# An mLSTM cell fused with a max-of-two MLP on one core: a hand-written engine order, the relu form, spread next-group work, and a denominator that is checked instead of applied

## Chip, cores, metric

One core of one Trainium2 chip. The metric is the device time of one execution in microseconds (us). A profile's span runs from the first to the last instruction of one execution; in these runs the device time is 1.6 to 2.2 us longer than the span of the same execution. Five engines work from their own queues, each in its own order: TensorE (PE in the profile, its weight loads PEld), VectorE (DVE), ScalarE (ACT), POOL, and SP, which issues most loads. PSUM is the memory in which the program puts TensorE's results, in banks. The granted clock is the share of TensorE's full clock that the profile records as let through; "half clock" is 0.5 of it. A run is called slow when its time is over 1.5% above that of the fastest run of the same kernel; comparisons use the fast runs.

## The reference, cut to what matters

```python
def _attn_ref(q, k, v, i_gate, f_gate, o_gate):        # 4 batches, 8 heads, 768 tokens, head size 40
    for t in range(S):
        m_new = np.maximum(f_gate[:, :, t] + m, i_gate[:, :, t])
        f_stab = np.exp(f_gate[:, :, t] + m - m_new); i_stab = np.exp(i_gate[:, :, t] - m_new)
        C = f_stab[..] * C + i_stab[..] * (v_t outer k_t)
        n = f_stab[..] * n + i_stab[..] * k_t
        denom = np.maximum(np.abs(n . q_t), 1.0)
        y[:, :, t] = sigmoid(o_gate) * (C q_t) / denom
def _moe_ref(x, w1, w2, w_out):                        # x: 3072 x 320, w1 and w2: 320 x 1024
    return np.maximum(x @ w1, x @ w2) @ w_out
```

## The kernel before

Only the first 64 tokens of each batch put anything into the state (a flag at the end checks it and starts a general path if not). So each batch has one small state, and every tile of 128 tokens is: transposes of q, four small matmuls (`ph`), the gate and the normaliser on VectorE and POOL (`y`), transposes of y (`py`). I call this the front of a tile. Four tiles make a group: `up` multiplies it by w1 - w2 in two halves, ScalarE takes the absolute value, and `out` sums the result. Since max(a, b) = (a + b)/2 + |a - b|/2, the half sum is folded into one small matrix Wc = (w1 + w2) w_out / 2. The framework's scheduler orders the instructions of every engine.

```python
def h_tile(b, c, P=None):
    ...                                            # four matmuls into ph
    nc.vector.tensor_scalar(out=den, in0=ph[:, :, D], scalar1=-1.0, scalar2=1.0, op0=OP.mult, op1=OP.max)
    nc.vector.tensor_tensor(out=den, in0=ph[:, :, D], in1=den, op=OP.max)
    nc.vector.reciprocal(out=rec, in_=den)
    nc.vector.tensor_tensor(out=t, in0=ph[:, :, 0:D], in1=sig[b][:, c], op=OP.mult)
    nc.gpsimd.tensor_tensor(out=y[:, 0:DM]..., in0=t, in1=rec..., op=OP.mult)
    nc.gpsimd.tensor_copy(out=y[:, DM:DM + 64], in_=y[:, DM - 64:DM])      # completes y
def moe_u(g, half):
    ...                                            # 8 full and 4 half-height matmuls of 512 columns
        nc.scalar.activation(out=gts[g][:, f:f + 2, :], in_=pus[lo], func=AF.Abs)
def moe_out(g, s):                                 # 3 matmuls with Wc, 8 with wo, copy, store
    ...
for g in range(1, NG + 1):
    for n in pairs: ...; front(n)                  # two pairs of tiles of group g
    for half in range(2):
        if g < NG: moe_u(g, half)
        for s in range(2): moe_out(g - 1, half * 2 + s)
# cut: loads, gates, state(b), weights, the check, the general path
```

## Time and profile before

| | before |
|---|---|
| device time, median of the first 3 runs | 136.48 us (136.3 to 137.49) |
| span of the profiled execution | 138.1 us |
| TensorE busy | 102.4 us, 74% |
| mean granted TensorE clock | 0.988 |

The table by stages comes first (kernel before). Its columns are the stretch, its length, the busy time of PE, PEld, DVE, ACT and POOL with the number of instructions, the granted TensorE clock, the DMA share and GB/s.

```profile
core 0: us, PE busy (x) PEld busy (x) DVE busy (x) ACT busy (x) POOL busy (x), PEclk, DMA share, GB/s
15.00:20.00 5.00, 2.39 (x17) 1.61 (x18) 5.00 (x5) 2.58 (x4) 4.03 (x3) 1.00 1.14 287
25.00:30.00 5.00, 2.75 (x26) 2.32 (x27) 3.78 (x12) 2.30 (x1) 3.98 (x7) 1.00 1.12 282
35.00:40.00 5.00, 4.95 (x37) 2.82 (x35) 4.00 (x9) 0.32 (x1) 0.98 (x3) 1.00 1.07 290
50.00:55.00 5.00, 2.99 (x19) 1.41 (x18) 2.01 (x9) 0.00 (x0) 3.06 (x7) 0.86 0.12 41
55.00:60.00 5.00, 4.65 (x23) 2.14 (x23) 0.62 (x3) 1.10 (x2) 0.00 (x0) 0.80 0.11 36
80.00:85.00 5.00, 4.53 (x44) 2.52 (x40) 2.89 (x11) 1.94 (x2) 1.88 (x4) 1.00 0.08 29
```

TensorE has little to do until 30 us while DMA runs at its limit; from 35 us on it is busy nearly all the time, but for the stretch around 50 to 60 us. The clock column starts at 1.00 only because no clock was recorded there (the record of this trace begins at 36.6 us): matmuls of 320 columns start 0.29 us apart at 32 us and 0.136 us apart later. The next lines are waits (waiting instruction, arrow, what ended the wait: total us, times, longest).

```profile
ACT L163 <- DMA ost<-in_o_gate_dram: 12.2, 1, 12.2
PEld L260 <- POOL y L250: 9.3, 16, 1.8
PE py L260 <- POOL y L250: 3.8, 8, 1.6
```

ScalarE's first table load stood 12.2 us behind its own DMA issues, which delayed the gates' exponentials to 13.5 us; their transposes then stood on TensorE until 18.8 us, behind transposes of weights that waited for POOL's sums. In the steady part TensorE waits for POOL's y. The last lines are TensorE's work in order of time (start, duration, instruction, count): some stalled y transposes and the first matmuls of `up` for groups 1 to 5.

```profile
32.09 2.31 PE L300 MATMUL pwc<-wo,wsT 128*128 128x320 bf16 x8
53.33 0.28 PE L260 MATMUL py<-ident_b,y 128*128 128x128 bf16 x2 [0.45 <-POOL y L250]
54.16 0.29 PE L260 MATMUL py<-ident_b,y 128*128 128x128 bf16 x1 [0.41 <-POOL y L252]
55.84 0.63 PE L315 MATMUL pu<-xT_165,wd 128*128 128x512 bf16 x1
74.22 1.89 PE L315 MATMUL pu<-xT_166,wd 128*128 128x512 bf16 x7
91.13 1.89 PE L315 MATMUL pu<-xT_167,wd 128*128 128x512 bf16 x7
105.28 1.89 PE L315 MATMUL pu<-xT_168,wd 128*128 128x512 bf16 x7
121.28 1.89 PE L315 MATMUL pu<-xT_169,wd 128*128 128x512 bf16 x7
```

From group 2 to group 5 the starts are 15.7 us apart on average, (121.28 - 74.22)/3.

### The profile page before, as it was taken

How to read it: one execution, taken by the hardware profiler on the slowest of the kernel's cores; microseconds unless marked ns; L12 is line 12 of the kernel's file. 1: busy time of each engine (PE TensorE's matmuls, PEld its weight loads, DVE VectorE, ACT ScalarE, POOL GpSimd, SP SyncE). 2: the span in 40 equal slices, each digit the busy share in tenths (PEclk: the TensorE clock that was granted, in tenths of full speed). 3: DMA queues.
4: the chain of work that ended last, by engine and by line, in shares of the span. 5: the costliest groups of instructions: out<-in, count | busy, mean ns of one | idle time of the engine just before them, and what ended most of it. 6: DMA issues, size and time to landing. Idle time of an engine off the chain costs nothing. (4 is left out here: it accounts for less than half of the span.)

```text
span 138.1 us, 2120 instructions
## 1 busy us (share of the span) xinstructions
PE 102.4 (74%) x761; PEld 57.4 (42%) x767; DVE 72.7 (53%) x196; ACT 37.4 (27%) x41; POOL 42.8 (31%) x87
## 2 busy tenths in 40 slices
PE   0000163568999876998899999997989999999870
PEld 0000042455734543345564445643654456543540
DVE  6980799767581992017694246634582156520220
ACT  0004820600059700055013550005500550014400
POOL 7530758794154026000541005414031005500000
PEclk9999999999999997799999999999999999999999
DMA  5999999999979911110112002110012101210041
GB/s 113 237 280 298 288 268 359 257 307 194 320 186 261 298 52 52 47 47 0 47 47 100 0 0 95 47 52 0 0 52 100 47 0 47 95 47 5 2 147 57
DMA packets 29407, 16.77 MB, mean 121 GB/s; under 512 B 17552, under 2 KB 28304, under 8 KB 29392
## 3 DMA queue, kind: packets, MB, share of 16 engines
q1 hardware_dynamic: 23152, 14.62, 37.1%
q10 hardware_dynamic: 6240, 1.97, 7.4%
q8 instruction: 8, 0.13, 0.4%
q14 instruction: 7, 0.06, 0.1%
HBM read 12.65 MB, written 3.93 MB: 120 GB/s over the span
## 5 line engine op out<-in xcount | busy, mean ns | idle before, releaser
L324 ACT ACTIVATE gt<-pu 128x1024 bf16<-128x1024 f32 x24 | 23.3, 1022 | 57.9 <-PE pu L320 57.9
L250 POOL TENSOR_TENSOR y<-t,rec 128x320 bf16<-128x320 f32 x24 | 17.3, 723 | 64.5 <-DVE den L244 45.1
L334 PE MATMUL po<-wo,gt 128*128 128x320 bf16 x192 | 33.7, 302 | 0.3 <-ACT gt L324 0.2
L334 PEld LDWEIGHTS <-gt 128*128 128x128 bf16 x192 | 17.5, 98 | 8.3 <-ACT gt L324 1.3
L336 DVE COPY o_sb<-po 128x320 f32<-128x320 f32 x24 | 11.2, 474 | 17.3 <-PE po L334 17.2
L282 PE MATMUL pw<-ident_b,ws 128*128 128x128 bf16 x16 | 2.6, 307 | 19.4 <-POOL ws L274 19.4
L260 PE MATMUL py<-ident_b,y 128*128 128x128 bf16 x72 | 11.8, 240 | 5.8 <-POOL y L250 3.8
L315 PEld LDWEIGHTS <-wd 128*128 128x128 bf16 x96 | 9.3, 99 | 12.1 <-issue 4.0
L206 DVE COPY qT<-pq 128x1024 bf16<-128x1024 bf16 x12 | 8.2, 686 | 7.5 <-PE pq L204 7.4
L260 PEld LDWEIGHTS <-y 128*128 128x128 bf16 x72 | 5.5, 104 | 14.8 <-POOL y L250 9.3
L248 DVE TENSOR_TENSOR t<-ph,sig 128x320 f32<-128x320 f32 x24 | 11.5, 481 | 0.0
L195 ACT ACTIVATE sig<-ost 128x960 f32<-128x960 f32 (+2 forms) x9 | 7.8, 917 | 9.3 <-issue 7.5
L282 PEld LDWEIGHTS <-ws 128*128 128x128 bf16 x16 | 1.4, 130 | 20.1 <-POOL ws L274 20.1
L236 PE MATMUL ph<-cq,qT 128*128 128x82 bf16 x80 | 6.0, 212 | 1.4 <-DVE qT L206 1.4
L252 POOL COPY y<-y 128x64 bf16<-128x64 bf16 x24 | 5.8, 240 | 1.5
L236 PEld LDWEIGHTS <-qT 128*128 128x128 bf16 x80 | 4.5, 105 | 3.6 <-DVE qT L206 2.3
L189 DVE CAST qb_128<-qst 128x960 bf16<-128x960 f32 x4 | 4.5, 1135 | 2.4 <-PE pq L204 2.4
L274 POOL TENSOR_TENSOR ws<-w_0_98,w_0_103 128x512 bf16<-128x512 f32 x2 | 3.4, 1726 | 6.6 <-DMA w_0_103<-in_moe_w_dram 6.6
L189 DVE CAST qb_127<-qst 128x960 bf16<-128x960 f32 (+2 forms) x5 | 5.2, 1037 | 0.3 <-DMA qst<-in_q_dram 0.3
L204 PE MATMUL pq<-ident_b,qb_127 128*128 128x128 bf16 x48 | 5.3, 265 | 0.0
L243 DVE TENSOR_SCALAR den<-ph 128x8 f32<-128x8 f32 x20 | 3.1, 160 | 4.0 <-PE ph L236 3.8
L274 DVE TENSOR_TENSOR wd<-w_0_98,w_0_103 128x512 bf16<-128x512 f32 x2 | 2.4, 1222 | 4.8 <-DMA w_0_103<-in_moe_w_dram 4.8
(110 smaller groups left out, 148.5 us busy)
## 6 DMA issues: line engine op xcount, KB each, us to landing
out_dram<-o_sb SPq DMA_DIRECT2D x24, 160.0 KB, 1.8
qst<-in_q_dram SPq DMA_DIRECT2D x3, 800.0 KB, 5.7
ost<-in_o_gate_dram SPq DMA_DIRECT2D x3, 800.0 KB, 7.3
wo_st<-in_moe_w_out_dram SPq DMA_DIRECT2D x1, 1280.0 KB, 6.9
w_0_98<-in_moe_w_dram SPq DMA_DIRECT2D x1, 512.0 KB, 5.3
w_0_103<-in_moe_w_dram SPq DMA_DIRECT2D x1, 512.0 KB, 7.6
w_1_110<-in_moe_w_dram SPq DMA_DIRECT2D x1, 512.0 KB, 7.4
w_1_115<-in_moe_w_dram SPq DMA_DIRECT2D x1, 512.0 KB, 5.7
```

What stands on the lines that cost most here:

```text
L189: eng.tensor_copy(out=qb[b % 2][:, c0:c1, :, 0:D], in_=qst[b][:, :, c0:c1, :].rearrange("p h c d -> p c h d"))
L195: nc.scalar.activation(out=sig[b][:, c0:c1], in_=ost[b][:, :, c0:c1, :].rearrange("p h c d -> p c h d"), func=AF.Sigmoid)
L206: nc.vector.tensor_copy(out=qT[b][:, c0:c0 + 2], in_=pq)
L236: nc.tensor.matmul(ph[:, 2 * p:2 * p + 2, :].rearrange("p a b -> p (a b)"), lhsT, rhs, start=True, stop=True)
L248: nc.vector.tensor_tensor(out=t, in0=ph[:, :, 0:D], in1=sig[b][:, c], op=OP.mult)
L250: nc.gpsimd.tensor_tensor(out=y[:, 0:DM].rearrange("p (h d) -> p h d", d=D), in0=t, in1=rec.unsqueeze(2).to_broadcast([128, H, D]), op=OP. ...
L252: nc.gpsimd.tensor_copy(out=y[:, DM:DM + 64], in_=y[:, DM - 64:DM])
L260: nc.tensor.transpose(py[:, c, j * L:(j + 1) * L], y[:, c * 128:(c + 1) * 128], ident_b)
L315: nc.tensor.matmul(pus[lo][:, j, :], wd[:, c, f * 128:(f + 1) * 128], x[:, c, :], start=(c == 0), stop=False)
L324: nc.scalar.activation(out=gts[g][:, f:f + 2, :], in_=pus[lo], func=AF.Abs)
L334: nc.tensor.matmul(po, gt[:, f, s * L:(s + 1) * L], wo[:, f, :], start=False, stop=(f == NFF - 1))
L336: nc.vector.tensor_copy(out=o_sb, in_=po)
```

## The change

Its parts: every engine's order is written by hand (`manual_schedule`), not left to the scheduler; max(a, b) = b + relu(a - b), so Wc = w2 w_out and POOL's sums become casts; the normaliser is no longer applied: the kernel only records n.q and checks at the end that |n.q| never exceeds 1, and takes the general path if it does, so what it saves holds only for inputs like these; next group's front is cut into six slots placed between `up` and the output tiles; 29 dummy matmuls fill early gaps to keep the clock up; the half-height matmuls of Wc run in pairs. Staging gets three buffers, and ScalarE issues only two loads.

```diff
+    order.enter_context(tc.manual_schedule())
+    idle(9)                                    # dummy matmuls; also idle(4) and idle(16)
-        nc.vector.reciprocal(out=rec, in_=den)
-        nc.gpsimd.tensor_tensor(out=y[:, 0:DM]..., in0=t, in1=rec..., op=OP.mult)
+        nc.vector.tensor_tensor(out=ys[n][:, 0:DM]..., in0=ph[:, :, 0:D], in1=ost[b][:, :, c, :], op=OP.mult)
+        nc.gpsimd.tensor_copy(out=ys[n][:, DM:DM + 64], in_=ys[n][:, DM - 64:DM])
+        nc.vector.tensor_copy(out=nqb[:, n, :], in_=ph[:, :, D])      # for the check
-            nc.scalar.activation(..., func=AF.Abs)
+            nc.scalar.activation(..., func=AF.Relu)
+    wc_mm()
+    start_batch(1)
+    for i in range(6):
+        slot(i, 0)                             # fronts of tiles 6 and 7, nothing between
     for g in range(1, NG + 1):
         for half in range(2):
             if g < NG:
-                moe_u(g, half)
-            for s in range(2):
-                moe_out(g - 1, half * 2 + s)
+                up(g, half)
+            if g == 1 and half == 1:
+                start_batch(2)                 # POOL: casts of q, first gate; ScalarE: sigmoids
+            out_rows(g - 1, half * 2)
+            slot(half * 3, g)
+            out_full(g - 1, half * 2)
+            slot(half * 3 + 1, g)
+            out_full(g - 1, half * 2 + 1)
+            slot(half * 3 + 2, g)
# cut: the slots' contents, loads, weights, the check
```

## The prediction

> **What bounds the kernel now.** Until about 37 us TensorE waits for loads and the prologue: the table by stages has it busy 2.4 to 2.8 us of each 5 us from 15 to 30 us, the DMA share is about 1.0 until 45 us, and the wait list shows ScalarE's first table load standing 12.2 us behind its own DMA issues. Matmuls run at half pace there (128x320 starts 0.29 us apart at 32 us, 0.136 later). From 37 to 133.6 us TensorE is the bound: 4.2 to 5.0 us busy of each 5, except around 50 to 55 us, where transposes wait for POOL's y and the granted clock then falls to 0.5 for 3.4 us. The last output copy starts at 133.7 us; the span ends at 138.1.
>
> **Floor of the steady part**, from start-to-start times in the timeline at full clock: an up half is 8 x 0.234 + 0.54 = 2.4 us; an output tile 11 x 0.136 = 1.5; a pair's q transposes 0.46, its ph matmuls 0.32, its y transposes 0.34 (six unstalled took that; three stalled took 0.36); state about 0.55 per batch. A group of four tiles with its successor's front is 4.8 + 6.0 + 2.2 + 0.4 = 13.4 us. The starts of up for groups 2 to 5 are 15.7 us apart: 2.3 us per group is stall.
>
> **What the change does.**
> - To y: den, max, reciprocal (about 0.5 us DVE a tile) and POOL's 0.72 us multiply go; DVE's 0.48 us multiply writes y at once. With fronts placed half a group ahead, y stalls should vanish: estimate 2 us per group, 8 us over four.
> - Relu should cost what Abs does on ScalarE (1.02 us), off the path. POOL's sums of weights become casts. Half-height Wc matmuls run in pairs; the switch eats what they save.
> - Prologue: gates ready near 8 us instead of 20.5; the first three pairs finish during the weight loads. Dummies keep the clock up; worth 1 to 2 us at most, since loads set that time.
> - Cost: output of group 0 now waits for up of group 1, which needs batch 1 loaded. Wo landed at 25 us; batch 1 is another 2.1 MB, at 272 GB/s (25 to 48 us) landing about 32.8 us. Sigmoid of its rest (about 1.6 us), y, transposes and copy put up of group 1 at about 37 us, against 55.8 before, with group 0's output still owed. TensorE idles several us before it, so its clock falls and the start loses about 2 us. The Trainium skill, "TensorE: Matmul & The Clock Gate", Part 1, says an idle window of about 3.4 us halves the clock; the trace's stretch at 0.5 has that length.
>
> **Sum.** 37 + 2 (cold) + 4 x 13.7 + 10.8 (up of group 5, output of 4) + 5.9 (last output) + 4.4 (tail, as now) = 115 us of profile span. Timed runs are about 1.2% below the profile (136.5 against 138.1): **113.5 us, 80% range 107 to 120**. Chances: faster over 2% 0.97, within 2% 0.02, slower 0.01.
>
> **Right if the profile shows:** gate transposes near 8 us; up of group 1 at 34 to 40 us, its y waiting for batch 1's ost; half clock just before; then up starts 13.4 to 14 us apart, TensorE 95% busy or more, no y waits; POOL under 30 us, DVE near 60.
>
> **Wrong if:** the fixed order makes TensorE wait for DVE (o_sb, qT, xT share one queue), groups staying above 14.5 us; batch 1 lands much later or earlier; the clock falls in mid-run; or POOL's casts of q hold the transposes.

## The result, and the profile after

| | before | after |
|---|---|---|
| device time, median (4 runs each) | 136.99 us (136.3 to 139.61) | 125.34 us (124.58 to 125.64) |
| span of the profiled execution | 138.1 us | 123.4 us |
| TensorE busy | 102.4 us, 74% | 103.7 us, 84% |
| VectorE, POOL busy | 72.7, 42.8 us | 57.7, 34.1 us |

The ratio of times is 0.916 (95% interval 0.911 to 0.922). Ratios here are the mean time of one kernel's fast runs over that of the other's of the same rounds, so not quite the ratio of the medians. The kernel is faster, but 12 us slower than predicted and outside the range.

The table by stages, kernel after:

```profile
15.00:20.00 5.00, 4.07 (x39) 2.66 (x37) 3.33 (x11) 1.14 (x2) 0.71 (x3) 1.00 1.07 303
35.00:40.00 5.00, 2.92 (x36) 2.15 (x34) 3.39 (x8) 2.22 (x3) 2.28 (x4) 1.00 1.10 330
40.00:45.00 5.00, 4.45 (x22) 1.86 (x22) 1.50 (x4) 0.00 (x0) 0.25 (x2) 0.66 1.14 234
50.00:55.00 5.00, 3.98 (x33) 2.06 (x31) 1.88 (x6) 3.00 (x4) 0.69 (x2) 1.00 0.09 33
55.00:60.00 5.00, 2.91 (x23) 1.96 (x24) 1.39 (x3) 0.72 (x1) 1.78 (x5) 0.85 0.10 36
85.00:90.00 5.00, 5.00 (x48) 3.40 (x45) 2.63 (x6) 1.94 (x2) 0.24 (x1) 1.00 0.10 34
```

The steady part is now full (85 to 90 us), the prologue fuller, and holes are left at 35 to 45 us and 50 to 60 us. TensorE's work in order of time, kernel after: Wc and then the way to `up` of group 1, and the starts of `up` for groups 2 to 5, then the half-height matmuls of the last group.

```profile
32.64 3.43 PE L321 MATMUL pwc<-wo,w2T 128*128 128x320 bf16 x24
36.81 0.61 PE L225 MATMUL pq<-ident_b,qb 128*128 128x128 bf16 x8 [0.36 <-DVE kT L234]
38.20 0.38 PE L247 MATMUL ps<-qT,kT 128*128 128x128 bf16 x4 [0.78 <-DVE qT L227]
39.37 0.33 PE L259 MATMUL ph<-vw,P 128*128 128x82 bf16 x4 [0.63 <-DVE P L249]
40.34 0.69 PE L275 MATMUL py<-ident_b,y 128*128 128x128 bf16 x6 [0.64 <-DVE y L262]
41.68 3.44 PE L335 MATMUL pu<-xT,wd 128*128 128x512 bf16 x8 [0.20 <-DVE xT L277]
60.77 2.46 PE L335 MATMUL pu<-xT,wd 128*128 128x512 bf16 x8
74.19 1.89 PE L335 MATMUL pu<-xT,wd 128*128 128x512 bf16 x8
89.14 1.89 PE L335 MATMUL pu<-xT,wd 128*128 128x512 bf16 x8
101.32 1.89 PE L335 MATMUL pu<-xT,wd 128*128 128x512 bf16 x8
112.51 0.29 PE L351 MATMUL po<-Wc_t,xT 64*128 64x320 bf16 x1 [0.34 <-DVE o_sb L362]
```

`up` of group 1 starts at 41.7 us after waits of 0.36, 0.78, 0.63, 0.64 and 0.20 us, and then takes 3.44 us for what takes 1.89 later: the clock is at half. The last line is from the last group: the second half-height matmul starts 0.65 us after the first, of which 0.34 us is waiting for VectorE to empty the PSUM bank into `o_sb` (runs 11, 12, 14 and 15 change that). The second hole, all engines in order of time, kernel after:

```profile
52.00 1.94 ACT L344 ACTIVATE gt<-pu 128x1024 bf16<-128x1024 f32 x2 [4.37 <-PE pu L340]
53.82 1.90 ACT L208 ACTIVATE ost<-ost 128x320 f32<-128x320 f32 x2
54.37 0.72 POOL L212 TENSOR_TENSOR ost<-ost,gT 128x320 f32<-128x320 f32 x1 [4.31 <-ACT ost L208]
55.04 1.38 POOL L204 CAST qb<-qst 128x640 bf16<-128x640 f32 x2
56.37 0.41 POOL L264 COPY y<-y 128x64 bf16<-128x64 bf16 x2
56.66 0.41 PE L275 MATMUL py<-ident_b,y 128*128 128x128 bf16 x4 [2.68 <-POOL y L264]
58.14 1.98 PE L360 MATMUL po<-wo,gt 128*128 128x320 bf16 x8
```

The y copies of tiles 10 and 11 wait in POOL's queue behind batch 2's gate multiply and casts, and that multiply waits for a sigmoid that stands behind the Relus on ScalarE. TensorE waits 2.68 us, and the output that follows takes 1.98 us where eight such matmuls take 1.25.

**Where the 14.7 us of span came from.** Before, at the start of `up` for group 2 (74.2 us) the output of groups 0 and 1 was done. After, at the same point (60.8 us) that of group 1 was still owed, about 5.9 us. So about 7.5 us come from before that point (74.2 - 60.8 - 5.9) and about 7.1 us from after it.

### The profile page after: what moved, and what is told of

Same layout as the page of the kernel before. It is cut to its first block, busy times and chain, and to the rows that moved or that the text cites. A ratio compares the mean times of both kernels' runs of the same rounds, so it can differ in the third digit from the quotient of the medians.

```text
span 123.4 us, 2122 instructions
## 1 busy us (share of the span) xinstructions
PE 103.7 (84%) x797; PEld 60.7 (49%) x797; DVE 57.7 (47%) x152; ACT 39.7 (32%) x47; POOL 34.1 (28%) x80
## 4 chain that ended last, share of the span: by engine, by line
PE 57%; DVE 4%; ACT 2%; POOL 2%; issue 1%; DVEq 0%
PE po L360 21%; PE pu L335 16%; PE po L358 5%; PE pu L340 4%; PE pq L225 3%; PE py L275 3%; PE ph L259 2%; DVE o_sb L362 2%; ACT gt L344 2%; PE po L351 1%; DVE xT L277 1%; POOL qb L204 1%; DVE y L262 1%; POOL ost L212 1%; PE pc L239 1%
## 5 line engine op out<-in xcount | busy, mean ns | idle before, releaser
L344 ACT ACTIVATE gt<-pu 128x1024 bf16<-128x1024 f32 x24 | 23.3, 1022 | 59.1 <-PE pu L340 59.1
L335 PE MATMUL pu<-xT,wd 128*128 128x512 bf16 x96 | 24.8, 405 | 1.4 <-DVE wd L289 1.2
L262 DVE TENSOR_TENSOR y<-ph,ost 128x320 bf16<-128x320 f32 x24 | 11.6, 487 | 18.2 <-PE ph L259 15.6
L165 PE MATMUL pd<-warm,ident_b 128*128 128x512 bf16 x29 | 9.5, 492 | 1.4 <-POOL ident_f masks.py:197 1.4
L225 PE MATMUL pq<-ident_b,qb 128*128 128x128 bf16 x96 | 8.8, 241 | 2.1 <-POOL qb L204 1.0
L358 PE MATMUL po<-Wc_t,xT 128*128 128x320 bf16 x48 | 10.5, 300 | 0.0
L204 POOL CAST qb<-qst 128x640 bf16<-128x640 f32 (+1 forms) x12 | 8.1, 696 | 5.9 <-DMA qst<-in_q_dram 5.7
L225 PEld LDWEIGHTS <-qb 128*128 128x128 bf16 x96 | 7.3, 110 | 3.3 <-issue 1.5
L208 ACT ACTIVATE ost<-ost 128x320 f32<-128x320 f32 (+1 forms) x8 | 7.7, 1001 | 3.3 <-DMA ost<-in_o_gate_dram 3.3
L277 DVE COPY xT<-py 128x768 bf16<-128x768 bf16 x12 | 6.6, 551 | 4.0 <-PE py L275 4.0
L340 PE MATMUL pu<-xT,wd 64*128 64x512 bf16 x48 | 7.3, 381 | 0.0
```

What stands on the lines that cost most here:

```text
L165: nc.tensor.matmul(pd[:, 0, :], ident_b, warm, start=True, stop=True)
L204: f(out=qb[b % 2][:, c0:c1, :, 0:D], in_=qst[b][:, :, c0:c1, :].rearrange("p h c d -> p c h d"))
L225: nc.tensor.transpose(pq[:, j, p, :], qb[b % 2][:, c + j, 2 * p:2 * p + 2, :].rearrange("p a b -> p (a b)"), ident_b)
L262: nc.vector.tensor_tensor(out=ys[n][:, 0:DM].rearrange("p (h d) -> p h d", d=D), in0=ph[:, :, 0:D], in1=ost[b][:, :, c, :], op=OP.mult)
L335: nc.tensor.matmul(pus[lo][:, j, :], wd[:, c, f * 128:(f + 1) * 128], x[:, c, :], start=(c == 0), stop=False)
L340: nc.tensor.matmul(pus[lo][:, j, :], wd2[r, half, j * 128:(j + 1) * 128], x[r, 2, :], start=False, stop=True)
```

## The experiments

The kernel after is the base of every run unless said. Each shares its rounds with the kernel before, so all are compared by that ratio: after stands at 0.916. The kernel before was itself not the same in all rounds: its median was 137.1 us in the rounds of runs 1 to 4 and 9 to 12, 137.4 in those of 5 to 8, and 139.0 in those of 13 to 15, where ratios therefore flatter by about 1%. The intervals reach 0.7 to 1.8 us to each side, so differences of 1 to 2 us between runs are at the edge of what this can tell. Every kernel gave a correct result.

### 1. The copy that completes y moves to VectorE

```diff
-        nc.gpsimd.tensor_copy(out=ys[n][:, DM:DM + 64], in_=ys[n][:, DM - 64:DM])
+        nc.vector.tensor_copy(out=ys[n][:, DM:DM + 64], in_=ys[n][:, DM - 64:DM])
```

> The 64-column copy that completes y goes from POOL to VectorE; nothing else changes. Theory A (the 2.7 us wait of the y transposes at 53.9 us comes from POOL's strict order: the copy stands behind batch 2's gate multiply and q casts; the half clock after it, 3.4 us, is a consequence): both go, the start of up for group 2 comes 4 us earlier, the time is 125.3 - 4 = 121 us. Theory B (VectorE's queue, with 24 more small copies, is the next limit, or another wait takes its place, such as batch 2's data): the time falls by less than 1.5 us.

Measured: 121.2 and 122.1 us in two fast runs, 127.2 and 129.2 us in two slow ones (ratio of fast runs 0.886). The wait at 53 us was gone, but the profile, of a slow run, showed a longer prologue. In it VectorE's copy stands still while POOL works. The first of two views is VectorE in order of time, of this run:

```profile
19.20 0.18 DVE L264 COPY y<-y 128x64 bf16<-128x64 bf16 x1
22.84 3.01 DVE L264 COPY y<-y 128x64 bf16<-128x64 bf16 x1
```

The second is POOL in order of time, of the same run:

```profile
22.58 1.06 POOL L448 MEMSET qb<- 128x1152 bf16 x1
23.57 1.38 POOL L449 MEMSET kblk<- 128x1536 bf16 x1
24.89 0.92 POOL L450 MEMSET vw<- 128x984 bf16 x1
```

0.18 us alone, 3.01 us when three POOL memsets run: the copy ends when they do. That such waits make the whole of the longer prologue (`up` of group 0 starts at 31.3 us, not 24.3) is likely and not shown. So this run does not decide; run 13 repeats it without that collision.

### 2. The slots of each half run together

```diff
             slot(half * 3, g)
-            out_full(g - 1, half * 2)
             slot(half * 3 + 1, g)
-            out_full(g - 1, half * 2 + 1)
             slot(half * 3 + 2, g)
+            out_full(g - 1, half * 2)
+            out_full(g - 1, half * 2 + 1)
```

> In each half group the three slots of next-group work run together before the two output tiles, not between them. Theory A (spreading hides the VectorE and POOL hops between TensorE steps): each half now exposes about 1.5 to 2 us, over eight halves with work 10 us or more: 135 us or above. Theory B (the queue of TensorE and two PSUM buffers would hide most of it anyway): below 129 us.

Measured: 133.8 us, ratio 0.975 (0.968 to 0.981). Near theory A: in a fixed order the spread is worth about 8 us.

### 3. The same program, ordered by the scheduler

```diff
-    order.enter_context(tc.manual_schedule())
```

> The hand-written order is given up: the same program, with the tool's own scheduler free to reorder, as in the kernel before. Theory A (the order itself carries most of the 11.6 us gain): 131 us or more, with y waits and up periods near 15 us. Theory B (less work per tile, earlier gates and staging carry it): within 3 us of 125.3.

Measured: **114.9 us**, ratio 0.837 (0.832 to 0.842). Both theories fall: the fixed order is not the gain, it costs 10.4 us. The starts of `up` for groups 1 and 2, TensorE, this run:

```profile
39.76 0.30 PE L359 MATMUL po<-wo,gt 128*128 128x320 bf16 x1
40.16 0.57 PE L359 MATMUL po<-wo,gt 128*128 128x320 bf16 x3
41.92 1.89 PE L334 MATMUL pu<-xT,wd 128*128 128x512 bf16 x8
53.03 1.89 PE L334 MATMUL pu<-xT,wd 128*128 128x512 bf16 x8
```

Group 1 starts no earlier (41.9 us), but output of group 0 (`po`) runs in the gaps before it, no half clock follows (the granted clock is 1.00 from 22.6 to 111 us), and group 2 starts at 53.0 us, not at 60.8.

### 4. The denominator applied again, in the hand-written order

```diff
+        nc.vector.tensor_scalar(out=den, ...); nc.vector.tensor_tensor(out=den, ...)
+        nc.vector.reciprocal(out=rec, in_=den)
-        nc.vector.tensor_tensor(out=ys[n]..., in0=ph[:, :, 0:D], in1=ost[b][:, :, c, :], op=OP.mult)
+        nc.vector.tensor_tensor(out=t, in0=ph[:, :, 0:D], in1=ost[b][:, :, c, :], op=OP.mult)
+        nc.gpsimd.tensor_tensor(out=ys[n]..., in0=t, in1=rec..., op=OP.mult)
# cut: the check of |n.q|, its copy per tile, and POOL's first multiply per batch (sig_first) go out
```

> The normaliser is computed and applied for each tile again (three VectorE operations, reciprocal, POOL multiply), in the hand-written order; the check of it goes. Theory A (as predicted: the long chain to y is what stalled transposes, 2 us per group): 125.3 + 8 or so = 133 us. Theory B (the spread slots hide the longer chain in the steady part, only the unhidden prologue, two batches deep, pays about 1.2 us per pair): 125.3 + 3 to 5 = 129 us.

Measured: 135.2 us in the one fast run, about 138 in three slow ones. That is about 10 us above after, so theory A, and more; with one fast run the size is rough. The edit lengthens the chain to y and also gives POOL more to do (47.4 us in place of 34.1); the two are not separated. Almost all of the change's gain over the kernel before is gone.

### 5. Wc woven into the fronts of tiles 6 and 7

```diff
-    wc_mm()
-    for i in range(6):
-        slot(i, 0)
+    f_k(1); wc_mm(0); f_c(1); f_q(6); wc_mm(1); f_s(1); f_h(7)
+    wc_mm(2); f_h(6); f_q(8); f_y(6)          # wc_mm(c): one of three blocks
```

One of Wc's copies also moves from ScalarE to VectorE.

> Hand-written order kept, but the three eight-matmul blocks of Wc are placed between the front steps of tiles 6 and 7, where TensorE stood idle; loads unchanged. Theory A (the start of up for group 1 at 41.7 us is set by a chain of front steps with nothing between them, after Wc, and by the clock that falls in its gaps): up starts near 38.5 us at full clock, the time is 125.3 - 4.5 = 121 us. Theory B (as predicted: batch 1's loads set it): start and time stay within 1 us.

Measured: 121.3 us, ratio of the three fast runs 0.883 (0.870 to 0.896). Theory A in time; `up` of group 1 starts at 39.8 us, not at the 38.5 that was expected. ScalarE's sigmoid of batch 1 also starts earlier, at 34.3 us in place of 36.4, since the Wc copies no longer stand before it; the run does not separate the two. TensorE at `up` of group 1, and at the second hole, which is untouched:

```profile
39.78 1.90 PE L335 MATMUL pu<-xT,wd 128*128 128x512 bf16 x7 [0.65 <-DVE xT L277]
53.23 0.61 PE L275 MATMUL py<-ident_b,y 128*128 128x128 bf16 x4 [2.67 <-POOL y L264]
```

### 6. An extra load ahead of batch 1

```diff
+    for j in range(4):
+        spare = outp.tile([128, DM], FP, name="o_sb", tag="o_sb")
+        nc.sync.dma_start(out=spare, in_=moe_w_out[128 * j:128 * j + 128])
     load_batch(1, nc.sync)
```

> Four extra loads of 164 KB (0.66 MB, about 2.4 us at 272 GB/s) go into the queue ahead of batch 1. Theory B (batch 1's loads bound the start of up for group 1): start and time 2.4 us later, 127.7 us. Theory A (the order's chain binds, the data lies waiting): under 0.7 us.

Measured: 125.8 us, ratio 0.919; `up` of group 1 starts at 42.15 us, 0.5 us later, not 2.4, and `up` of group 0 was already 0.5 us later in this execution (24.76 against 24.30). Theory A: loads did not set that start. The loads were delayed indeed: the last one of batch 1 landed at 36.0 us in place of 32.4. ScalarE in order of time, kernel after, shows where its data lay waiting:

```profile
36.11 0.43 ACT L322 CAST Wc_t<-pwc 128x320 bf16<-128x320 f32 x1 [1.75 <-PE pwc L321]
36.43 1.90 ACT L208 ACTIVATE ost<-ost 128x320 f32<-128x320 f32 x2
```

The sigmoids of batch 1 start only after Wc's last copy, 4 us after their data.

### 7. No dummies

```diff
-    idle(9)
-    idle(4)
-        if half == 0:
-            idle(16)
-        else:
+        if half == 1:
```

> All 29 dummy matmuls are taken out. As predicted (worth 1 to 2 us, since loads bound the prologue): 125 to 127.5 us. Rival: prologue matmuls are on the chain, and without dummies they run at half clock until about 36 us (up of group 0 twice 1.9 us, Wc 3.4, transposes 1 us): 125.3 + 6 to 8 = 132 us. Third: the 16 before up of group 0 only delay it: 124 us.

Measured: 125.8 us, ratio 0.916, the same as after. Without dummies the first `up` half runs at half clock (3.2 us in place of 1.9) but starts 1.4 us earlier, at 22.9 us; what the dummies win they had cost. The second half starts at 29.6 us (29.0 with dummies), in both after 1.18 us of waiting for VectorE or ScalarE to prepare its weights. Nor did the first 13 dummies always keep the clock up: in the profiles of runs 5, 6 and 13 it is recorded at half from 8 or 9 us to 18 or 19 us.

### 8. The Abs form put back

```diff
-            f(out=w2b[:, c, half * 512:half * 512 + 512], in_=t[:, 1, c])
+            G.tensor_tensor(out=w2b[:, c, ...], in0=t[:, 0, c], in1=t[:, 1, c], op=OP.add)
-            A.copy(out=wo[:, 0:4], in_=wo_st[:, 0:4])
+            A.activation(out=wo[:, 0:4], in_=wo_st[:, 0:4], func=AF.Copy, scale=0.5)
-            nc.scalar.activation(..., func=AF.Relu)
+            nc.scalar.activation(..., func=AF.Abs)
```

> The Abs form is put back in the hand-written order: POOL adds w1 and w2 (1.3 to 1.7 us per 128x512) where ScalarE and POOL cast w2; wo is halved in its cast; Relu becomes Abs. Theory A (the relu form shortens the prologue, since sums on POOL hold the transposes before Wc): 3 to 6 us slower, 129 us. Theory B (sums hide behind other prologue waits): within 1.5 us of 125.3.

Measured: 127.2 us, ratio 0.927 (0.916 to 0.939). About 1.5 us slower; the interval reaches down to no difference. It falls between the two theories. In its profile Wc starts at 35.2 us, not 32.6.

### 9 and 10. Denominator applied, and slots bunched, both in the scheduler's order

The edits are those of runs 4 and 2, with `manual_schedule` taken out as in run 3.

> Denominators applied per tile again (as in the fourth run) and the scheduler free to reorder (as in the third, 114.9 us). Theory A (the long chain to y costs what it adds wherever no other TensorE work is ready; a scheduler cannot hide it, as in the kernel before): 121 us or more. Theory B (with free order the chain is hidden, and the 10 us it cost in the hand-written order was that order's inflexibility): 118 us or less.

> Slots of next-group work written together in the program (as in the second run, 133.8 us), the scheduler free to reorder. Theory A (the spread in the text matters only because a fixed order keeps it): within 2 us of 114.9. Theory B (the scheduler follows the text's order closely, so the spread is worth its 8.5 us here too): 121 us or more.

Measured: 123.5 us, ratio 0.901 (0.896 to 0.905), for the denominator; 116.4 us, ratio 0.850 (0.845 to 0.855), for the bunched slots. The denominator costs 8.7 us of 137 in the scheduler's order too (0.901 - 0.837), so neither of the two orders hides it; that is theory A of run 9. The spread, worth 8 us in the fixed order, is worth about 1.8 us when the scheduler may move things (0.850 - 0.837); that is theory A of run 10.

### 11. Three mends at once

Runs 1 and 5 together, and in the last group:

```diff
-            out_rows(g - 1, half * 2)                  # half-height matmuls of both tiles
+            out_rows(g - 1, half * 2, (0,) if g == NG else (0, 1))
...
+            if g == NG: out_rows(g - 1, half * 2, (1,))
             out_full(g - 1, half * 2 + 1)
```

> The hand-written order with three mends: Wc woven into the fronts of tiles 6 and 7 (4 us alone), the copy that completes y on VectorE (3.5 us alone), and in the last group the half-height matmuls of one tile at a time, so that the second does not wait 0.65 us twice for a PSUM bank (1.3 us). If the three causes are separate and complete: 125.3 - 8.8 = 116.5 us, up starts of groups 1 and 2 about 14 us apart. If the half-clock stretches have another cause, or mends overlap: 119 us or more.

Measured: 123.7 us median, 121.5 and 123.1 us in fast runs, two slow ones (ratio of fast runs 0.903). A miss: the prologue had grown again. `up` of group 0 starts at 28.7 us, not 24.3, with copies of 0.9 us on VectorE beside POOL's work.

### 12. The scheduler's order without dummies

Run 3, with run 7's edit and the last group's half-height matmuls one tile at a time.

> The scheduler's order (114.9 us), without the dummies and with the last group's half-height matmuls one tile at a time. Dummies bought nothing in the hand-written order; in the scheduler's their 12 us of TensorE time stands among real work until 23 us. Theory A (loads and chain bind the prologue): 113 to 115 us. Theory B (the clock matters here, where up of group 0 and Wc are followed by output at once): 116.5 us or more.

Measured: **112.4 us**, ratio 0.822 (0.816 to 0.827), the fastest kernel. The two edits together are worth about 2 us (0.837 - 0.822); they are not separated. Runs 14 and 15 show no worth of dummies in the hand-written order.

### 13. The copy on VectorE only from tile 8 on

```diff
-        nc.gpsimd.tensor_copy(out=ys[n][:, DM:DM + 64], ...)
+        (nc.vector if n >= 8 else nc.gpsimd).tensor_copy(out=ys[n][:, DM:DM + 64], ...)
```

> As the first run, but the completing copy moves to VectorE only for tiles 8 to 23; the prologue keeps POOL. Theory A (POOL's queue holds y of tile 11 behind batch 2's work, and the half clock follows from that idle stretch; the first run's longer prologue came from VectorE and POOL in each other's way): prologue as before (up of group 1 near 42 us), no wait of 2.7 us, up of group 2 near 56.5 us, all runs at 125.3 - 4 = 121.3 us, no slow ones. Theory B (the wait moves elsewhere or VectorE copies slow the groups): above 123.5 us.

Measured: 121.1 us, ratio 0.878 (0.868 to 0.888), all four runs fast. Theory A. `up` of group 1, the y transposes and `up` of group 2:

```profile
42.40 1.89 PE L335 MATMUL pu<-xT,wd 128*128 128x512 bf16 x7 [0.20 <-DVE xT L277]
52.88 0.50 PE L275 MATMUL py<-ident_b,y 128*128 128x128 bf16 x6
56.07 1.89 PE L335 MATMUL pu<-xT,wd 128*128 128x512 bf16 x7
```

No wait before the transposes, no half clock after them; group 1 takes 13.7 us (56.07 - 42.40), as the prediction had it. But the first line shows luck as well: the half clock at `up` of group 1 is missing too, though nothing before it was changed. By their mean clocks, two of the four executions most likely had it (0.943; 121.6 and 122.0 us) and two did not (0.956; 120.4 and 120.6 us). The first two are the ones to set against the three executions of after with both half clocks (125.2 to 125.6 us): the copy is worth about 3.7 us, and the rest of the 4.2 is where the clock's windows fell.

### 14 and 15. The mends together without the collision, with and without dummies

Runs 5 and 13 and the last group's edit of run 11; run 15 also without dummies.

> The three mends together (Wc woven in, copy on VectorE from tile 8 on, last group's half-height matmuls one by one), dummies kept. If the three causes are separate and complete: 125.3 - 4.0 - 4.0 - 1.3 = 116 us. If they overlap or another wait appears: 119 us or more.

> The same without dummies. Theory A (dummies buy and cost nothing, as in the hand-written order before): within 1 us of the run with them. Theory B (they delay: the 16 before up of group 0 end 1.3 us after its weights are ready; as the scheduler's order gained about 2 us without them): 1 to 2 us faster.

Measured: 116.9 us, ratio 0.845 (0.836 to 0.853), and 117.1 us, ratio 0.846 (0.836 to 0.855). The times add up within 1 us: 125.3 - 4.0 - 4.2 - 1.3 would be 115.8. The 1.3 us for the last group is read from the trace (0.65 us twice) and was never run alone, and run 14's profile has no half clock at `up` of group 1. Dummies again make no difference: theory A of run 15.

## Why the prediction was right or wrong

Right:

- **Direction and the steady groups.** Groups 2 to 4 take 13.5 us on average ((101.32 - 60.77)/3) against 15.7 before; 13.7 was forecast. One by one they take 13.4, 15.0 and 12.2 us, where 13.4 to 14 was forecast for each. TensorE is busy 97% of that time, and no group of them waits for y as before.
- **The denominator.** Runs 4 and 9 put it, chain to y and POOL's multiply together, at about 9 us in either order; 8 us was forecast for the steady groups alone.
- **Dummies and Relu.** "Worth 1 to 2 us at most" was an upper bound; run 7 shows nothing. Relu takes what Abs took (1022 ns each in the groups of both profiles).

Wrong, term by term (span, forecast against the profile):

| term | forecast | measured | difference |
|---|---|---|---|
| start of `up`, group 1 | 37 | 41.7 | +4.7 |
| half clock at that start | 2 | 1.55 (3.44 - 1.89) | -0.45 |
| group 1, without that | 13.7 | 17.5 (60.77 - 41.68 - 1.55) | +3.8 |
| groups 2 to 4 | 41.1 | 40.6 | -0.5 |
| group 5, last output and tail | 21.1 | 22.1 (123.4 - 101.3) | +1.0 |
| span to device time | -1.5 | +2.1 (125.5 - 123.4) | +3.6 |

1. **"Another 2.1 MB ... put up of group 1 at about 37 us."** The loads came as forecast (batch 1 landed at 32.4 us, 32.8 was expected). The step that failed is the path from there to `up`, 4.2 us by the forecast and 9.3 us in the profile: it was counted as if sigmoid, y and transposes followed the landing at once. The order put the sigmoids behind Wc's copies on ScalarE, and the fronts of tiles 6 and 7 after Wc as a chain of short TensorE steps, each waiting for a VectorE step. Run 6 delays the loads by 3.6 us and hardly anything moves; run 5 leaves them alone, weaves Wc in, and gets 4 us: 1.9 us by an earlier start (39.8 us) and most of the rest by the half clock that stays away. Why even that start is 2.8 us after the forecast was not tested.
2. **"With fronts placed half a group ahead, y stalls should vanish."** True for VectorE's part, not for POOL's queue in group 1. I had read the slots on TensorE and not what `start_batch(2)` puts ahead of the copy in POOL's order. Run 13 takes the copy out of that queue and gets about 3.7 us, wait and half clock together (4.2 with the luck told there). The last "wrong if" item came close (POOL's casts of q), but put the harm on q's transposes and no time on it; POOL's sum, 34.1 us for "under 30", was short as well.
3. **The clock.** The forecast expected the half clock at the start of group 1, and it came in the profiled execution of after. It need not come: run 13 has the same gaps there without it. The Trainium skill, "TensorE: Matmul & The Clock Gate", Part 1, says the clock is set by a free-running activity window of 3413 ns. The trace agrees: the recorded half-clock stretches are 3.413 us or 2 or 3 times that, but for the one with which each record ends. What I missed is the second one (58.5 to 61.9 us), which follows the 2.7 us wait.
4. **"Timed runs are about 1.2% below the profile."** This took the 138.1 us profile for a typical execution. Where runs list both, the device time is 1.6 to 2.2 us above the span of the same execution, and the kernel before has spans of 134.8 to 136.6 us in the rounds of runs 1 to 4. The profiled execution was one of the slower ones (the slowest timed one was 139.6 us). Its mean clock of 0.988, with the half-clock stretch at 53 us, is not that of most executions: 9 of the 28 in the rounds of runs 1 to 15 show 0.988 or less (spans of 137.0 to 139.6 us), the others 0.991 to 1.0.
5. **The name of the change.** I let the hand-written order count as the carrier of the gain, placing fronts half a group ahead. Run 3 shows that the order as a whole costs 10.4 us; in its trace other output runs in the waits of point 1, which a fixed queue leaves empty. Its placement helps when frozen (run 2), but most of that is what freezing had cost (run 10). Mended by hand it comes within 2 us of the scheduler (run 14 against run 3), but run 3 lacks the mend of the last group. Like against like, without dummies and with that mend, the fixed order still costs 3 to 5 us (run 15 against run 12: 0.846 and 0.822 of about 137 us by the ratios, 117.1 and 112.4 us by the times); what holds those is not shown. That run 3 lands near my 113.5 us is partly chance: the term of point 4 had the wrong sign.

Open: how run 12's two edits share their 2 us, and why half of the executions in runs 1 and 11 were slow. The profile of run 1 shows 24 us at half clock, of which 10 us, before 19.4 us, stand in the fast profile of run 13 as well, but why it differs between executions was not tested.

## What to carry to other kernels

Before crediting a fixed order, run the same program with the scheduler free: it is one line, and it separates less work from where the work stands. When an order is fixed, check every engine's queue for small copies that TensorE needs standing behind bulk work for the next stage, since POOL's and ScalarE's queues stall as surely as TensorE's. Take the span and the device time from the same execution before turning one into the other.

## What the Trainium skill lacked or had wrong

- "TensorE: Matmul & The Clock Gate", Part 1, gives half clock, in its table, after at least one idle window of about 3.4 us. Here a sparse window was enough: in the 3.41 us before 41.43 us of the kernel after, where the half clock begins, TensorE did about 1.3 us of work by start-to-start times (mostly transposes, which Part 4 of the page says count differently). The page gives no share of work at which the clock falls, and no run here settles it: the window from 36.39 to 39.80 us of run 13 holds about 1.4 us, more of it matmuls that are not transposes, and full clock followed.
- The same page, Part 4, gives about 275 ns for a 128x128 bf16 transpose in a kernel. The length of one is near that (217 to 241 ns in the kernel after). But it also says that full clock does not engage for them, and their pace here follows the clock: eight take 0.45 us from start to start at full clock (from 73.74 us, 0.056 us each) and 0.85 us at half clock (from 59.92 us).
- "SBUF — State Buffer", "Who interferes with whom", says a VectorE copy in a two-port mode and POOL block each other for the whole instruction. Run 1 is in line with that, though the trace does not tell the copy's mode, and shows more: a 128x64 copy took 3.01 us in place of 0.18, across three POOL memsets in a row. That a queue of instructions holds the other off for its whole length is not said there.
- No page measures what dummy matmuls in the gaps of a real kernel are worth; here the ratio is 0.916 with 29 of them and without.
